# Four paddings between matmul operands in SBUF, in a fused retention, maxout and bilinear kernel

## The chip, the cores and the metric

The kernel runs on one core of one Trainium2 chip. The metric is device time in microseconds (us) for one launch, the median of several runs. An effect of under 0.5%, about 6.35 us here, can't be told from no change by such runs.

## The reference, cut to what matters

```
scores = (q @ k^T) / sqrt(64), decayed by gamma_h ** (i - j) for j <= i     # 8 batches, 8 heads, 576 positions, width 64
x = scores @ v                          -> [4608, 512]
h = max(x @ w1, x @ w2, x @ w3)         -> [4608, 768]     (first products)
z = h @ w_out                           -> [4608, 512]
g = (z @ u1) * (z @ u2)                 -> [4608, 1024]
out = g @ (u3 @ u_out)                  -> [4608, 512]     (the kernel folds u3 and u_out into one matrix, w4)
```

The inputs are float32, the weights come as 64-bit words. Each float32 operand is split into a high and a low part in the matmul type float32r, and a product is three matmuls: high by high, low by high, high by low.

## The kernel before

The work runs in stages, and TensorE (PE) has matmuls in nearly all of it:

- 0 to 569 us: attention by chunks of 64 or 128 positions, mixed with the **first products** (line 486). A first product is 12 matmuls of 128x128 weights (the stationary operand, `w1h` and `w1l`, pool `w1`) against 512 columns of `xh` and `xl` (the moving operand, pools `x0` to `x2`). 166 products make 1992 matmuls, 1896 of them 512 columns wide and 96 (the halved ones at the start) 256 wide. `ORDER` and the due times of `when` set the sequence.
- 569 to 698 us: **z** in seven products per group of tokens (a Strassen-like scheme, `Z_ORDER`), stationary `zp["w"]` (`za11h` and so on), moving `hh`, `hl` from a ring of three (line 772, `product` at line 709). Four groups are 512 wide (504 matmuls), the last is 256 wide (126 matmuls) and reads columns 48 to 304 of its tiles (`columns`, line 116).
- 698 to 896 us: **the fold of the last two weights into w4** (192 matmuls of 512 columns into `ps_w`, stationary `th`, `tl`, moving `oh`, `ol`, pool `t34`), then the products for g (`ps_x`, `ps_v`, `ps_y`, stationary the sums in `wsum`, moving `ops`): 1344 matmuls of 512 columns and, from 897 to 936 us, 336 of 256 columns.
- 1089 to 1264 us: **the output products**, 1512 matmuls of 256 columns, stationary the pieces of g, moving the pieces of w4.

Tiles lie in SBUF where their pools put them: a pool's tiles follow each other in the order in which they are first asked for, pools on the left side grow upward and on the right side downward. Nearly all tiles of operands are a whole number of 256 bytes per partition, so all stationary operands of a stage share one remainder of the address modulo 256, and all moving ones another. Below, the **offset** of a matmul is the start of the weights loaded for the next matmul less the start of its own moving operand, modulo 256. In the program as built before the change it is 0 for all first products, for z and for the fold into w4 at 512 columns and for the products for g at 512 columns; it is 64 for the last group of z, the last group of the products for g and all output products. Three places of the code set it already: `skew(o_p, 352)` at line 801, `columns`, and the `skew` of 32 or 64 bytes at line 1034.

Of the kernel before, what the change touches and what calls it, by code (L numbers as in the profile page):

```python
# [9 lines left out]
F32 = mybir.dt.float32  # L10
# [12 lines left out]
P = 128  # L23
# [64 lines left out]
def tile_retention_maxout_bilinear(ctx: ExitStack, tc, a, out):  # L88
# [3 lines left out]
    def copy_r(dst, src):  # L92
        nc.scalar.activation(dst, src, AF.Copy)  # L93

    def low(eng, dst, full, hi):
        eng.tensor_tensor(dst, full, hi.bitcast(F32), ALU.subtract)  # L96
# [13 lines left out]
    g_d = [dram.tile([P, KF2, N1], F32, name=f"g_d{t}") for t in range(NT // N1)]  # L110
    w4_d = dram.tile([P, KF2, DM], F32, name="w4_d")

    def skew(pool, size):
        pool.tile([P, size // 4], F32, name="skew")

    def columns(size):
        at = 0 if size == N1 else 48
        return slice(at, at + size)
# [2 lines left out]
        return ps_mm.tile([P, 512], F32, tag="mm", name=name)  # L121

    left = ctx.enter_context(ExitStack())
    hb_p = left.enter_context(tc.tile_pool(name="hb", bufs=4, side="left"))
    w1_p = left.enter_context(tc.tile_pool(name="w1", bufs=1, side="left"))
    x_p = {2: left.enter_context(tc.tile_pool(name="x2", bufs=1, side="left"))}
    cv_x = ctx.enter_context(ExitStack())
    x_p.update({t: cv_x.enter_context(tc.tile_pool(name=f"x{t}", bufs=1, side="left")) for t in range(2)})
    cv = cv_x.enter_context(tc.tile_pool(name="cv", bufs=2, side="left"))
# [372 lines left out]
    for t in range(n_blk):  # L502
        for f in range(KF1):
            for i in range(3):
                k = T_BLK * t + 3 * f + i
                if t < EARLY:
                    split = t == 0 and 3 * f + i < HALVED
                    for e, cols in enumerate(halves if split else (whole,)):
                        name = f"{t}.{3 * f + i}" + "ab"[e] * split
# [12 lines left out]
    zp = {}  # L522
# [7 lines left out]
    def splitter(pool, src, hi, lo, eng, tag, bufs):  # L530
        raw = pool.tile([P, hi.shape[-1]], F32, tag=tag, name=tag, bufs=bufs)
        load(raw, src)

        def split():
            copy_r(hi, raw)
            low(eng, lo, raw, hi)

        return split

    def open_z():  # L540
        right.close()
        cv_x.close()
        zp["ps"] = ctx.enter_context(tc.tile_pool(name="ps_2", bufs=2, space=PSUM, side="right"))
        p = zp["p"] = bx.enter_context(tc.tile_pool(name="zp", bufs=1, side="right"))
        zp["w"] = {x: [p.tile([P, KH, half], F32R, name=f"z{x}{v}") for v in "hl"] for x in AN}

    def raw_h(tag, bufs=1):
        return zp["p"].tile([P, KH, N1], F32, tag=tag, name=tag, bufs=bufs)
# [56 lines left out]
    def split_h(n):  # L605
        j, n = divmod(n, len(Z_ORDER))
        if j < len(z_groups):
            x = Z_ORDER[n][1]
            raw, size = hr[j, x], z_groups[j][3]
            hh, hl = hq[j, n] = [zp["p"].tile([P, KH, N1], F32R, tag=f"h{v}", name=f"h{v}", bufs=Z_RING)[:, :, columns(size)] for v in "hl"]  # L610
            copy_r(hh, raw)
            low(nc.vector, hl, raw, hh)

    t_last = T_BLK * (n_blk - 1)
    when(t_last, open_z)
    for c, tag in enumerate(("T3", "T2", "b21")):
        for n, step in enumerate(z_weights(c, tag)):
# [7 lines left out]
    for n in range(Z_RING):  # L625
        when(t_last + 13.6 + n, split_h, n)
    when(t_last + 15.2, load_h, 1, "b11")

    with tc.manual_schedule():
# [88 lines left out]
        t34, w3t, wo2 = {}, {}, {}  # L718
# [4 lines left out]
            return splitter(t34["p"], flat(w3t_d[:, k, 4 * e:4 * e + 4]), *map(flat, w3t[n]), nc.vector, "raw34", 3)  # L723

        def get_wo2(k):
            wo2[k] = [t34["p"].tile([P, DM], F32R, tag=x, name=x) for x in ("oh", "ol")]
            return splitter(t34["p"], wo2_d[:, k], *wo2[k], nc.gpsimd if k % 2 else nc.vector, "raw34", 3)

# [2 lines left out]
        def prepare_34(*gets):  # L731
            for split in pending:
                split()
            pending[:] = [get(n) for get, n in gets]

        first_34 = [((get_w3t, 0), (get_wo2, 0)), ((get_w3t, 1),), ((get_w3t, 2), (get_wo2, 1)), ()]

        def open_34():
            t34["p"] = t34x.enter_context(tc.tile_pool(name="t34", bufs=2, side="left"))

        zo_p = bx.enter_context(tc.tile_pool(name="zo", bufs=1, side="right"))

# [16 lines left out]
        for j, (_, _, _, size) in enumerate(z_groups):  # L759
            Z = {}  # L760
            saved = {}
            for n, (x, y) in enumerate(Z_ORDER):
                bank_of = "XVXYXYX"[n]
                fresh = bank_of not in Z
                if fresh:
                    Z[bank_of] = [bank8(f"ps_{bank_of}{i}") for i in range(2)]
                ps = Z[bank_of]
                ah, al = zp["w"][x]
                bh, bl = hq.pop((j, n))
                for i in range(2):  # L770
                    ms = slice(i * P, i * P + P)
                    product(ps[i][:, :size], [(ah[:, c, ms], al[:, c, ms], bh[:, c], bl[:, c]) for c in range(KH)], fresh, True, not fresh)
                for i in range(2):
                    if n in (0, 2, 3):
                        saved[n, i] = snap_z(ps[i], size)
                    elif n == 6:
                        keep_z(j, 2 + i, 0, ps[i])
                    else:
                        keep_z(j, *{1: (i, 0), 4: (2 + i, 1), 5: (i, 1)}[n], ps[i], saved.pop(({1: 0, 4: 3, 5: 2}[n], i)))
                split_h(j * len(Z_ORDER) + n + Z_RING)  # L780
                for fn, dj, *args in behind_z[n]:
                    fn(j + dj, *args)
                if steps and n in (2, 3, 5, 6):
                    steps.pop(0)()
            if j == 3:
                for step in steps:
                    step()
                sx.close()
                open_34()
                steps = [lambda gets=gets: prepare_34(*gets) for gets in first_34]  # L790
# [8 lines left out]

        ops = [operand_set(o_p, 0)]  # L800
        skew(o_p, 352)
        behind = []

# [79 lines left out]
        for n in range(2 * KF2):  # L883
            k, e = divmod(n, 2)
            th, tl = w3t.pop(n)
            for m in range(4 * e, 4 * e + 4):
                if k == 0:
                    ps_w.append(bank8(f"ps_w{m}"))
                product(ps_w[m], [(th[:, m % 4], tl[:, m % 4], *wo2[k])], k == 0, k == KF2 - 1)
                if k == KF2 - 1:  # L890
                    t = w4_p.tile([P, DM], F32, tag="w4", name="w4")
                    copy_r(t, ps_w[m])
                    load(w4_d[:, m], t)
            prepare_34(*[(get_w3t, n + 3)] * (n + 3 < 2 * KF2), *[(get_wo2, k + 2)] * (e == 1 and k + 2 < KF2))
            lows()
            if steps:
                steps.pop(0)()
# [120 lines left out]
        def g_steps(s):  # L1018
# [13 lines left out]
            def split(x, eng):  # L1032
                if s in (0, 3) and not ops:
                    skew(gpool[s % 2], 32 if s else 64)
                h, l = ops[x] = [gpool[s % 2].tile([P, 4, P], F32R, tag=f"{x}{v}", name=f"{x}{v}") for v in "hl"]
                src = w[x]
                copy_r(h, src)
                if s:
                    low(eng, l, src, h)
                else:  # L1040
                    behind.append(lambda: low(eng, l, src, h))
# [58 lines left out]
        for n, (k, q) in enumerate(visits):  # L1100
            B, size = ops[k % 2], z_groups[k][3]
# [190 lines left out]
```

## Time and profile before

| | |
|---|---|
| median of 3 runs | 1270.91 us (1267.66 to 1272.45) |
| the profiled execution's own time | 1266.24 us |
| its span, first to last instruction | 1264.5 us |
| PE busy | 1256.5 us, 99% of the span |
| granted TensorE clock | 1.000 in the mean: 2.4 GHz throughout |
| DVE, ACT, POOL busy | 882.8, 487.2, 314.5 us |

How to read it: matmuls are pipelined, so a row's length ("mean ns of one") is longer than the distance from one matmul's start to the next. In an undisturbed stretch of matmuls of one shape the length less about 162 ns is that distance. A weight load (LDWEIGHTS, engine PEld) has rows of its own, and runs beside the matmul before the one it serves.

### The profile page before, as it was taken

What the parts mean: (1) busy time and instruction counts of PE and PEld (TensorE: products, weight loads), DVE (VectorE), ACT (ScalarE), POOL (GpSimd) and SP (SyncE); (2) the same over time, 40 slices, a digit from 0 to 9 for tenths busy, and PEclk for the clock granted to TensorE, in tenths of its full rate; (3) what the DMA queues carried; (4) which work ended last, traced back from release to release, by engine and by line L of the source; (5) the groups of instructions that cost most, each with busy time, mean ns of one, the idle gap of its engine ahead of it and who ended that gap; (6) DMA issues with size and microseconds to landing.
All of it is one profiled execution on the core that took longest, in us unless ns stands there. A gap on an engine that the chain in (4) does not pass through costs nothing.

```text
span 1264.5 us, 22993 instructions
## 1 busy us (share of the span) xinstructions
PE 1256.5 (99%) x8900; PEld 1078.9 (85%) x8900; DVE 882.8 (70%) x1256; ACT 487.2 (39%) x873; POOL 314.5 (25%) x262
## 2 busy tenths in 40 slices
PE   9999999999999999999999999999999999999999
PEld 6888888888888888888888788888998888999998
DVE  5985666666666766366898446776666766899896
ACT  4541122222222222234565354443344343455554
POOL 2201211211111110000000314544243542344443
PEclk9999999999999999999999999999999999999999
DMA  9945787787878895434743643333333315355553
GB/s 219 239 115 118 151 221 195 184 213 177 239 183 177 179 197 148 159 108 166 226 158 125 219 128 121 122 119 108 106 113 133 117 51 162 131 175 159 168 174 101
DMA packets 323793, 199.34 MB, mean 158 GB/s; under 512 B 241634, under 2 KB 279266, under 8 KB 323684
## 3 DMA queue, kind: packets, MB, share of 16 engines
q1 hardware_dynamic: 323684, 197.87, 56.7%
q8 instruction: 70, 1.15, 0.4%
q14 instruction: 39, 0.32, 0.1%
HBM read 131.76 MB, written 66.06 MB: 156 GB/s over the span
## 4 chain that ended last, share of the span: by engine, by line
PE 94%; DVE 3%; DMA 2%; ACT 1%; issue 1%; SPq 0%; POOL 0%; DVEq 0%; ACTq 0%; POOLq 0%
PE ps_h L486 35%; PE ps_x L715 23%; PE ps_y L715 11%; PE ps_v L715 6%; PE ps_X L715 5%; PE sc L369 3%; PE o L384 3%; PE ps_w L715 2%; PE ps_Y L715 2%; PE st L404 1%; PE ps_V L715 1%; PE o L391 1%; DMA raw<-w3t_d 1%; DMA a<-wp_d 1%; PE kp L345 0%
## 5 line engine op out<-in xcount | busy, mean ns | idle before, releaser
L486 PE MATMUL ps_h<-xh,w1h 128*128 128x512 f32 (+1 forms) x664 | 257.5, 389 | 0.0
L486 PE MATMUL ps_h<-xh,w1l 128*128 128x512 f32 (+1 forms) x664 | 254.4, 385 | 0.4 <-DVE w1l L96 0.4
L486 PE MATMUL ps_h<-xl,w1h 128*128 128x512 f32 (+1 forms) x664 | 174.2, 384 | 0.0
L486 PEld LDWEIGHTS ps_h<-xh,w1h 128*128 128x128 f32 x664 | 124.6, 188 | 27.6 <-issue 2.1
L486 PEld LDWEIGHTS ps_h<-xh,w1l 128*128 128x128 f32 x664 | 124.8, 188 | 24.7 <-DVE w1l L96 0.6
L486 PEld LDWEIGHTS ps_h<-xl,w1h 128*128 128x128 f32 x664 | 123.0, 188 | 24.8
L496 DVE TENSOR_TENSOR hb<-ps_h,hb 128x512 f32<-128x512 f32 (+1 forms) x110 | 74.4, 676 | 97.5 <-PE ps_h L486 92.6
L1146 POOL TENSOR_TENSOR c<-c 128x512 f32<-128x512 f32 (+1 forms) x60 | 83.4, 1391 | 176.7 <-DVE c L1138 123.3
L1133 ACT ACTIVATE snap<-ps_x 128x512 f32<-128x512 f32 (+1 forms) x100 | 55.5, 555 | 176.5 <-PE ps_x L715 175.7
L355 POOL TENSOR_TENSOR q<-q,tables 128x512 f32<-128x512 f32 (+1 forms) x31 | 31.4, 1012 | 276.4 <-DMA q<-in_q_dram 209.1
L93 ACT ACTIVATE hb<-ps_h 128x512 f32<-128x512 f32 (+1 forms) x56 | 32.5, 580 | 148.9 <-PE ps_h L486 139.1
L166 ACT ACTIVATE e<-raw 128x512 f32<-128x512 f32 x64 | 42.8, 669 | 105.8 <-DMA raw<-in_moe_w_dram 67.3
L93 ACT ACTIVATE xh<-o 128x512 fp32r<-128x512 f32 (+1 forms) x40 | 22.2, 554 | 118.8 <-PE o L391 76.9
L96 POOL TENSOR_TENSOR ol<-raw,oh 128x512 fp32r<-128x512 f32 x4 | 6.5, 1636 | 239.5 <-DVE tl L96 219.0
L358 POOL TENSOR_TENSOR v<-v,tables 128x512 f32<-128x512 f32 x40 | 44.6, 1117 | 59.9 <-DMA v<-in_v_dram 55.3
L376 DVE TENSOR_TENSOR p<-sc,mask 128x512 f32<-128x512 f32 (+1 forms) x80 | 48.0, 627 | 11.8 <-PE sc L369 11.7
L1138 DVE TENSOR_TENSOR c<-ps_x,snap 128x512 f32<-128x512 f32 (+1 forms) x40 | 25.2, 637 | 38.8 <-PE ps_x L715 15.9
L172 DVE CUSTOM_DVE_ANT_0 m<-m,r 128x1024 uint16<-128x1024 uint16 x64 | 47.0, 735 | 6.9
L1138 DVE TENSOR_TENSOR c<-ps_v,snap 128x512 f32<-128x512 f32 (+1 forms) x40 | 25.0, 635 | 35.2 <-PE ps_v L715 19.7
L715 PE MATMUL ps_x<-t4h,a 128*128 128x512 f32 (+1 forms) x160 | 45.5, 368 | 0.3 <-DVE a L96 0.3
L715 PE MATMUL ps_x<-b11h,a 128*128 128x512 f32 (+1 forms) x160 | 45.2, 367 | 0.0
L715 PE MATMUL ps_y<-b22h,s 128*128 128x512 f32 (+1 forms) x160 | 45.2, 367 | 0.0
(299 smaller groups left out, 3262.5 us busy)
## 6 DMA issues: line engine op xcount, KB each, us to landing
zr<-g_d SPq DMA_DIRECT2D x18, 1024.0 KB, 6.1
raw<-in_moe_w_dram SPq DMA_DIRECT2D x34, 512.0 KB, 5.7
g_d<-c SPq DMA_DIRECT2D x64, 256.0 KB, 2.1
zr<-z_d SPq DMA_DIRECT2D x28, 512.0 KB, 6.2
h_d<-hb SPq DMA_DIRECT2D x54, 256.0 KB, 3.4
b<-h_d SPq DMA_DIRECT2D x16, 768.0 KB, 6.6
out_dram<-ob SPq DMA_DIRECT2D x35, 256.0 KB, 2.0
v<-in_v_dram SPq DMA_DIRECT2D x32, 256.0 KB, 4.2
```

Of the source, the lines that this page charges most:

```text
L93: nc.scalar.activation(dst, src, AF.Copy)
L166: nc.scalar.activation(z["e"], raw[:, :, 1].bitcast(F32), AF.Copy, scale=2.0 ** -112)
L172: nc.vector.tensor_tensor(z["m"], z["m"], z["r"], ALU.add)
L358: nc.gpsimd.tensor_tensor(z["v"], z["v"], vd.unsqueeze(2).to_broadcast([P, H, D]), ALU.mult)
L369: nc.tensor.matmul(z["sc"][g][keys, h, :c], z["kt"][rows, h, keys], z["qt"][rows, h, :c], start=True, stop=True)
L376: nc.vector.tensor_tensor(z[g][:c, :, :c], z["sc"][g][:c, :, :c], mask[:c, :c].unsqueeze(1).to_broadcast([c, G, c]), ALU.mult)
L486: nc.tensor.matmul(ps[:, cols], l, r, start=n == 0, stop=n == len(mms) - 1)
L496: nc.vector.tensor_tensor(hb, ps[:, cols], hb, ALU.max)
L715: nc.tensor.matmul(ps, l, r, start=start and j == 0, stop=stop and j == len(mms) - 1, skip_group_check=again)
L1133: nc.scalar.activation(t, ps[:, :size], AF.Copy)
L1138: nc.vector.tensor_tensor(r, ps[:, :size], t, ALU.add)
L1146: nc.gpsimd.tensor_tensor(x, x, y, ALU.mult)
```

## The change

`skew` makes a dummy tile that moves the tiles behind it. It gets a numbered name and one buffer (`bufs=1`), and is called in six new places, in the pools `w1`, `x2`, `zp` (twice) and `t34` (twice):

```
--- before.py
+++ after.py
-    def skew(pool, size):
-        pool.tile([P, size // 4], F32, name="skew")
...
     left = ctx.enter_context(ExitStack())
+    skews = []
+
+    def skew(pool, size):
+        skews.append(pool.tile([P, size // 4], F32, name=f"skew{len(skews)}", bufs=1))
+
     hb_p = left.enter_context(tc.tile_pool(name="hb", bufs=4, side="left"))
     w1_p = left.enter_context(tc.tile_pool(name="w1", bufs=1, side="left"))
+    skew(w1_p, 192)
     x_p = {2: left.enter_context(tc.tile_pool(name="x2", bufs=1, side="left"))}
+    skew(x_p[2], 64)
...
         zp["w"] = {x: [p.tile([P, KH, half], F32R, name=f"z{x}{v}") for v in "hl"] for x in AN}
+        skew(p, 192)
...
             hh, hl = hq[j, n] = [zp["p"].tile([P, KH, N1], F32R, tag=f"h{v}", name=f"h{v}", bufs=Z_RING)[:, :, columns(size)] for v in "hl"]
+            if j == 0 and n == 0:
+                skew(zp["p"], 96)
...
         def get_wo2(k):
+            if k == 0:
+                skew(t34["p"], 192)
             wo2[k] = [t34["p"].tile([P, DM], F32R, tag=x, name=x) for x in ("oh", "ol")]
...
         def open_34():
             t34["p"] = t34x.enter_context(tc.tile_pool(name="t34", bufs=2, side="left"))
+            skew(t34["p"], 64)
```

In the program as built, the offsets become:

| matmuls | count | offset before | after |
|---|---|---|---|
| first products, 512 and 256 columns | 1896 and 96 | 0 | 192 (64 below) |
| z, 512 columns | 504 | 0 | 64 |
| z, last group, 256 columns | 126 | 64 | 128 |
| fold into w4, 512 columns | 192 | 0 | 64 |
| products for g, 512 and 256 columns | 1344 and 336 | 0 and 64 | the same |
| output products, 256 columns | 1512 | 64 | the same |

No instruction is added, removed or moved: on every engine and on SP's queue the built programs hold the same operations in the same order with the same waits. Only addresses in SBUF differ.

## Rows read from the trace of the kernel before

**Rows 1.** The page: busy time by engine, granted clock, chain that ended last.
```profile
PE 1256.5 (99%) x8900; PEld 1078.9 (85%) x8900; DVE 882.8 (70%) x1256; ACT 487.2 (39%) x873; POOL 314.5 (25%) x262
...
PEclk9999999999999999999999999999999999999999
...
PE 94%; DVE 3%; DMA 2%; ACT 1%; issue 1%; SPq 0%; POOL 0%; DVEq 0%; ACTq 0%; POOLq 0%
PE ps_h L486 35%; PE ps_x L715 23%; PE ps_y L715 11%; PE ps_v L715 6%; PE ps_X L715 5%; PE sc L369 3%; PE o L384 3%; PE ps_w L715 2%; PE ps_Y L715 2%; PE st L404 1%; PE ps_V L715 1%; PE o L391 1%; DMA raw<-w3t_d 1%; DMA a<-wp_d 1%; PE kp L345 0%
```

**Rows 2.** Groups by line and shape, whole span: 512 columns.
```profile
line engine op names shapes xcount | busy us, mean ns | idle before us <-releasers
L486 PE MATMUL ps_h<-xh,w1h 128*128 128x512 f32 x632 | 248.8, 394 | 0.0
L486 PE MATMUL ps_h<-xh,w1l 128*128 128x512 f32 x632 | 246.2, 390 | 0.0
L486 PE MATMUL ps_h<-xl,w1h 128*128 128x512 f32 x632 | 169.0, 389 | 0.0
...
L715 PE MATMUL ps_w<-oh,th 128*128 128x512 f32 x64 | 25.2, 394 | 0.3 <-ACT oh L93 0.3
```

**Rows 3.** Groups by line and shape, 509 to 568 us: first products.
```profile
L486 PE MATMUL ps_h<-xh,w1h 128*128 128x512 f32 x88 | 34.3, 389 | 0.0
```

**Rows 4.** Groups by line and shape, 571 to 683 us: z.
```profile
L715 PE MATMUL ps_V<-hh,za12h 128*128 128x512 f32 x24 | 9.3, 389 | 0.0
```

**Rows 5.** Groups by line and shape, 42.2 to 44 us: halved first products.
```profile
L486 PE MATMUL ps_h<-xh,w1l 128*128 128x256 f32 x6 | 1.5, 283 | 0.0
L486 PE MATMUL ps_h<-xl,w1h 128*128 128x256 f32 x7 | 1.2, 283 | 0.0
```

**Rows 6.** Groups by line and shape, 684 to 697 us: z's last group.
```profile
L715 PE MATMUL ps_X<-hh,zs3l 128*128 128x256 f32 x6 | 1.7, 281 | 0.0
```

**Rows 7.** Groups by line and shape, 897 to 925 us: last group for g.
```profile
L715 PE MATMUL ps_x<-t2h,s 128*128 128x256 f32 x24 | 4.4, 281 | 0.0
```

**Rows 8.** Groups by line and shape, 927 to 936 us: the same matmuls, later.
```profile
L715 PE MATMUL ps_v<-b21h,a 128*128 128x256 f32 x8 | 1.4, 276 | 0.0
```

**Rows 9.** Groups by line and shape, 1112 to 1260 us: output products.
```profile
L715 PE MATMUL ps_x<-wt,s3h 128*128 128x256 f32 x64 | 13.5, 276 | 0.0
```

**Rows 10.** Busy time by stretch: us, each engine's busy us (instructions), clock, DMA share, GB/s.
```profile
897.00:925.00 28.00, 28.00 (x241) 28.00 (x240) 20.73 (x38) 13.58 (x32) 7.46 (x9) 1.00 0.18 62
...
940.00:1088.00 148.00, 148.00 (x654) 122.57 (x653) 102.54 (x129) 63.09 (x115) 62.53 (x42) 1.00 0.33 110
1089.00:1100.00 11.00, 11.00 (x95) 11.00 (x94) 8.71 (x15) 4.88 (x10) 2.33 (x2) 1.00 0.43 144
1112.00:1260.00 148.00, 148.00 (x1308) 148.00 (x1307) 128.05 (x166) 78.89 (x168) 65.42 (x46) 1.00 0.49 156
```

**Rows 11.** Timeline, 247.3 to 248 us: start, duration, engine; a first product before attention.
```profile
247.13 0.61 PE L486 MATMUL ps_h<-xl,w1h 128*128 128x512 f32 x2
247.13 0.19 PEld L486 LDWEIGHTS ps_h<-xl,w1h 128*128 128x128 f32 x1
...
247.67 0.43 PEld L404 LDWEIGHTS st<-v,kn 128*64 128x64 f32 x12 [0.35 <-issue]
```

**Rows 12.** Groups by line and shape, 247.55 to 247.65 us: the last of those alone.
```profile
L486 PE MATMUL ps_h<-xl,w1h 128*128 128x512 f32 x1 | 0.4, 388 | 0.0
```

**Rows 13.** Timeline of PE, 124 to 128.5 us: first products after attention.
```profile
126.25 0.50 PE L486 MATMUL ps_h<-xh,w1h 128*128 128x512 f32 x1
126.58 0.39 PE L486 MATMUL ps_h<-xh,w1l 128*128 128x512 f32 x1
126.81 0.40 PE L486 MATMUL ps_h<-xh,w1h 128*128 128x512 f32 x1
```

## Prediction

> **What bounds the kernel now.** I read the page first, then the groups by line and shape, then stretches of time. PE is busy for 99% of the span at the full clock, 2.4 GHz in every slice, and the chain that ended last is PE for 94%, the first products alone for 35% [rows 1]. So time comes or goes only with the distance from one matmul to the next, and the reader is to look at lengths of matmuls. At 512 columns they are 389 ns in the first products and in z [rows 3, 4]. At 256 columns there are three lengths: 283 ns in the halved first products (offset 0), 281 ns in z's last group and at first in g's last group (offset 64), and 276 ns later in that group and in the output products (offset 64 too) [rows 5 to 9]. How a length stands to a distance: from 940 to 1088 us there are 654 matmuls in 148.00 us, about 227 ns apart, and from 1112 to 1260 us 1308, about 113 ns apart [rows 10]; the lengths there are 389 and 276, both 162 to 163 more. So 281 and 283 mean 5 and 7 ns more per matmul than 276.
>
> **What the offset did so far.** Rows 5 to 9 are what speaks for such paddings: with offset 0 a 256-column matmul took 7 ns over the shortest, with offset 64 either 5 ns over or nothing. Which of the two it is does not follow from the offset alone, since g's last group has both with the same offsets [rows 7, 8]. A weight load is 0.19 us long [rows 11]: at 256 columns, 113 ns apart, there is always one under way, at 512 columns, 227 ns apart, there is time without one.
>
> **The change part by part.** The change moves no instruction and no wait, so it has one term only: a price per matmul times the matmuls whose offset changes. These are 1896 first products, 504 of z and 192 of the fold into w4 at 512 columns, 2592 together, and at 256 columns 96 first products and 126 of z.
>
> *512 columns, what can be gained.* If a clash between the weight load and the moving operand were in the 389 ns, a matmul without a weight load beside it would be shorter. The trace has such matmuls: where attention takes over, the last first product has nothing beside it. In rows 11 a pair of them begins at 247.13, so the second begins 0.23 us later at 247.36, and the next weight load comes only at 247.67, 0.31 us behind that start [rows 11]. It is 388 ns long [rows 12], against 389 with a load [rows 3]. So at offset 0 the load costs 1 ns, and the most that a better offset can give is 2592 x 1 ns = 2.6 us. The columns themselves are the rest: 388 less 276 is 112 ns for 256 more columns, so 512 columns take about 224 ns with no load near.
>
> A rule of the Trainium skill bears on this (TensorE: Matmul & The Clock Gate, section "Step-by-step: what each phase is for"): loading the next weights takes no SBUF read bandwidth from the running matmul, since PE reads the two through separate ports. By that rule every offset is as good as another and the sum is 0. The 1 ns at 512 columns agrees with it; the 5 and 7 ns at 256 columns don't, so it isn't taken for granted for new offsets.
>
> *512 columns, what can be lost.* No row shows 512 columns at an offset of 64 or 192. The nearest rows are the 256-column ones, with 5 and 7 ns. For the 696 of z and of the fold (offset 64) the rows at that offset give 0 or 5 ns: 0 to 3.5 us. For the 1896 first products (offset 192) there is no row at all: 0 to 7 ns, or 0 to 13.3 us. I take 0 for both: at 512 columns the load ends long before the matmul, so what it loses in a clash can be made up within the same matmul, and the long stretches at 512 columns show that PE falls into the undisturbed distance of 227 ns by itself after a few matmuls. That can be seen behind each pause: the first is 0.50 us long, the next ones 0.39 to 0.40 [rows 13], and in the quiet stretch at the end it is 389 for all [rows 3].
>
> *After a pause.* The first products' groups have 394, 390 and 389 ns in the mean over the span [rows 2], 632 x (5 + 1) ns = 3.8 us over 389. There are 22 returns from attention, and the first matmul of each is 0.11 us longer, 2.4 us, because its follower's weights are loaded late; padding doesn't touch this. What is left, 1.4 us, is the few matmuls that settle. Another offset may shorten or lengthen this: -1.4 to +1.4 us, taken as 0.
>
> *256 columns.* The 96 halved first products go from 283 to an unknown length, at best 276: -0.7 us at most, and much of that is hidden since PE waits for weights there. z's last group goes from 281 to 276 at best, 126 x 5 = -0.6 us, or to 283, +0.3 us. Taken as 0.
>
> *What isn't padded but may follow.* g's last group begins at 281 and the output products too: 241 and 95 matmuls [rows 7, 10]. If they inherit another rhythm from the stage ahead and begin at 276, that is -1.2 and -0.5 us. Taken as 0.
>
> Sum: 0. Against the profiled execution that is 1266.2 us again (span 1264.5 and 1.7 us around it). That execution lies 4.7 us below the median of the runs, so as a time to be measured I take the median, **1270.9 us**. All gains together are 2.6 + 1.4 + 0.7 + 0.6 + 1.2 + 0.5 = 7.0 us, to 1263.9; the losses that still belong to this case are 3.5 us (z and the fold at 5 ns), 1.4 and 0.3: 5.2 us, to 1276.1.
>
> **The rivals.**
>
> *The first products clash at 192 (slower).* The mechanism: at 64 below, the weight load of the next matmul and the moving operand meet in a way that repeats in each matmul, as at 256 columns with offset 0, where it doesn't go away, and PE never reaches the distance of 227 ns. For it: at 256 columns the offset does matter, and 64 below is a place that no row covers. Against it: the slack at 512 columns, and the 1 ns. Its price is 1896 x 5 to 7 ns = 9.5 to 13.3 us, 1280.4 to 1284.2; with z and the fold in the same state 2592 x 5 to 7 = 13.0 to 18.1 us, 1283.9 to 1289.0. It decides from 6.35 us / 1896 = 3.4 ns per first product.
>
> *What lies over 2.4 GHz is clash after all (faster).* 512 columns at 2.4 GHz are 213 ns, the rows show 227, and if all of the 14 ns over that came from operands that meet and the new offsets ended it, 2592 x 14 = 36 us would go: 1235 us. Against it stands the 388 ns of the matmul without a load, and that 256 columns more take 112 ns where 2.4 GHz would make 107. It would need the lone matmul to be slowed by something else. [...]
>
> *The change doesn't do what it says.* The built program has the offsets of the text, so this is left as: the relation modulo 256 between these two starts is not what made 283, 281 and 276. Then nothing moves, which is the forecast's time.
>
> **How the numbers follow.** Forecast (no offset matters at 512 columns by more than 1 to 2 ns): 0.58, 1270.9 us, its own range 1263.9 to 1276.1. Slower by the first products' clash, with or without the others: 0.36, 1280 to 1289. Faster by over 0.5%: 0.06, nearly all of it the second rival or several small gains at once. What a measurement can tell from no change is about 0.5%, 6.35 us. The range runs from 1264, all small gains, to 1284, the upper price of the clash in the first products alone; outside it are the cases of all three stages at 7 ns and of the large gain.
>
> **What would show it.** Right: the first products' groups stay at 388 to 390 ns in a quiet stretch, z's and the fold's at 389, PE's lone matmul before attention at 388, DVE, ACT and POOL as before, the clock 2.4 GHz throughout. The clash: the first products' three groups at 394 to 396 in the stretch that now has 389, with PE's idle time unchanged and the whole difference between 0 and 569 us. The gain: 375 to 378 there. A different length in z than in the first products would show that the sign of the offset counts. The forecast is wrong if any 512-column group moves by over 3 ns; it is right for a wrong reason if two groups move against each other.

## The result: 0.6% slower, and the profile after

| | before | after |
|---|---|---|
| median of the runs taken side by side | 1268.12 us (11 runs, 1264.33 to 1272.45) | 1273.9 us (11 runs) |
| ratio after to before, 95% interval | | 1.0056 (1.0034 to 1.0078) |
| profiled execution, and its span | 1266.24, 1264.5 us | 1278.55, 1276.8 us |

One execution of after, at 1791.95 us, and one of before, at 5968.75 us beside the last two whole kernels below, were disturbed and are left out of the ratios and spreads. The other ten of after lie between 1271.79 and 1280.1 us. The kernel became slower, by little more than a measurement can tell; the forecast was no change.

The page of after: busy time by engine, granted clock in 40 slices, chain that ended last by engine.

```profile
PE 1268.9 (99%) x8900; PEld 1084.6 (85%) x8900; DVE 885.8 (69%) x1256; ACT 489.1 (38%) x873; POOL 312.3 (24%) x262
...
PEclk9999999999999999999999999999999999999999
...
PE 97%; DVE 2%; DMA 1%; ACT 1%; issue 0%; POOL 0%; ACTq 0%; DVEq 0%; POOLq 0%
```

Against [rows 1] PE is busy 12.4 us longer with the same 8900 instructions, and the span is 12.3 us longer; DVE, ACT and POOL are within 3 us of what they were, and the clock is 2.4 GHz throughout. So the time lies in PE's own distances. The groups by line and shape tell where, here in quiet stretches (515 to 565 us, 600 to 680, 684 to 697, 725 to 750, 800 to 890, 1120 to 1268); the matmuls of L486 and L715 stand at L491 and L723 in after.

```profile
L491 PE MATMUL ps_h<-xh,w1h 128*128 128x512 f32 x74 | 29.0, 392 | 0.0
L491 PE MATMUL ps_h<-xh,w1l 128*128 128x512 f32 x74 | 28.9, 391 | 0.0
...
L723 PE MATMUL ps_V<-hh,za12h 128*128 128x512 f32 x18 | 7.1, 396 | 0.0
...
L723 PE MATMUL ps_X<-hl,zs2h 128*128 128x256 f32 x6 | 1.7, 282 | 0.0
...
L723 PE MATMUL ps_w<-ol,th 128*128 128x512 f32 x37 | 14.6, 396 | 0.0
...
L723 PE MATMUL ps_y<-b22h,s 128*128 128x512 f32 x40 | 12.3, 389 | 0.0
...
L723 PE MATMUL ps_x<-wt,s2h 128*128 128x256 f32 x64 | 13.9, 281 | 0.0
```

The first products went from 389 to 391 and 392 [rows 3], z from 389 to 396 [rows 4], z's last group from 281 to 282 [rows 6], the fold into w4 reads 396 too. The products for g, whose offset did not change, still read 389. The last row is the surprise: the output products, not touched by the change, read 281 where they read 276 [rows 9]. The counts in equal stretches say the same. Here are the stretches of 50, 80, 25 and 148 us by busy time, first of after, then of before (first bracket: PE's matmuls).

```profile
515.00:565.00 50.00, 50.00 (x220) 41.03 (x219) 26.75 (x51) 13.89 (x29) 0.00 (x0) 1.00 0.43 143
600.00:680.00 80.00, 80.00 (x344) 64.51 (x343) 70.94 (x64) 45.61 (x53) 0.00 (x0) 1.00 0.53 175
725.00:750.00 25.00, 25.00 (x109) 20.13 (x108) 15.24 (x18) 12.58 (x23) 6.98 (x5) 1.00 0.47 141
...
1112.00:1260.00 148.00, 147.78 (x1256) 147.58 (x1255) 128.66 (x167) 78.18 (x165) 65.39 (x45) 1.00 0.50 160
```

```profile
515.00:565.00 50.00, 50.00 (x222) 41.39 (x222) 27.86 (x50) 14.91 (x31) 0.00 (x0) 1.00 0.46 154
600.00:680.00 80.00, 80.00 (x355) 66.26 (x354) 72.97 (x67) 45.53 (x53) 0.00 (x0) 1.00 0.55 178
725.00:750.00 25.00, 25.00 (x112) 20.68 (x111) 12.03 (x18) 13.95 (x25) 3.48 (x2) 1.00 0.48 154
```

80 us hold 344 matmuls of z where they held 355, and 148 us hold 1256 output products where they held 1308 [rows 10]. From here on I give the **distance** from one matmul's start to the next, taken from the records in stretches without a pause. The stages, by the start of each stage's first matmul in the two profiled executions:

| stage | us before | us after | difference | distances before and after, ns |
|---|---|---|---|---|
| until the first full product | 49.24 | 47.63 | -1.6 | |
| first products, mixed with attention | 519.98 | 524.49 | +4.5 | 227.1, 229.0 |
| z, 512 columns | 114.74 | 117.71 | +3.0 | 226.7, 233.3 |
| z, last group | 14.84 | 14.96 | +0.1 | 117.8, 118.7 |
| fold into w4 | 45.73 | 46.13 | +0.4 | 227.5, 233.3 |
| products for g | 344.41 | 344.42 | 0.0 | 226.7, 226.7 (512 columns) |
| output products to the end | 175.59 | 181.50 | +5.9 | 113.3, 117.8 |

The table adds up to the 12.3 us. Stages that are the same also differ between profiled executions: with the first products at offset 0 that stage took 520.0, 520.4, 520.6 and 522.1 us in four kernels, and z at offset 0 114.5 to 115.9. So single differences of the table carry 1 to 2 us, and the distances are the steadier measure. By distances times matmuls the changed offsets are worth 1873 x 1.93 = 3.6 us in the first products (those that another follows at once), 504 x 6.67 = 3.4 in z, 192 x 5.8 = 1.1 in the fold, 0.1 in z's last group: **8.2 us**. The stages of the table give 4.5 + 3.0 + 0.1 + 0.4 = 8.0. The -1.6 at the start and the +5.9 at the end remain. The start took 47.5 to 49.2 us in the eight profiled executions of whole kernels here, before and after lie near its two ends, and no run tells whether the padding has a part in that. The experiments had to tell whether the +5.9 belongs to the change.

### The profile page after: what moved, and what is told of

Same layout as the page of the kernel before. It is cut to its first block, busy times and chain, and to the rows that moved or that the text cites. A ratio compares the mean times of both kernels' runs of the same rounds, so it can differ in the third digit from the quotient of the medians.

```text
span 1276.8 us, 22993 instructions
## 1 busy us (share of the span) xinstructions
PE 1268.9 (99%) x8900; PEld 1084.6 (85%) x8900; DVE 885.8 (69%) x1256; ACT 489.1 (38%) x873; POOL 312.3 (24%) x262
## 4 chain that ended last, share of the span: by engine, by line
PE 97%; DVE 2%; DMA 1%; ACT 1%; issue 0%; POOL 0%; ACTq 0%; DVEq 0%; POOLq 0%
PE ps_h L491 35%; PE ps_x L723 23%; PE ps_y L723 11%; PE ps_X L723 6%; PE ps_v L723 6%; PE ps_Y L723 3%; PE ps_w L723 3%; PE sc L374 3%; PE o L389 3%; PE ps_V L723 1%; PE st L409 1%; PE o L396 1%; DMA raw<-w3t_d 1%; PE kp L350 0%; DVE zr L1055 0%; PE qp L350 0%
## 5 line engine op out<-in xcount | busy, mean ns | idle before, releaser
L491 PE MATMUL ps_h<-xh,w1h 128*128 128x512 f32 (+1 forms) x664 | 258.5, 391 | 0.0
L491 PE MATMUL ps_h<-xh,w1l 128*128 128x512 f32 (+1 forms) x664 | 255.4, 386 | 0.0
L491 PE MATMUL ps_h<-xl,w1h 128*128 128x512 f32 (+1 forms) x664 | 175.7, 386 | 0.0
L491 PEld LDWEIGHTS ps_h<-xh,w1h 128*128 128x128 f32 x664 | 124.7, 188 | 28.6 <-issue 2.1
L491 PEld LDWEIGHTS ps_h<-xh,w1l 128*128 128x128 f32 x664 | 124.8, 188 | 25.3
L491 PEld LDWEIGHTS ps_h<-xl,w1h 128*128 128x128 f32 x664 | 123.0, 188 | 25.9
L180 DVE SCALAR_TENSOR_TENSOR m<-raw,m 128x512 int32<-128x512 int32 x64 | 45.8, 720 | 0.2
L723 PE MATMUL ps_x<-t4h,a 128*128 128x512 f32 (+1 forms) x160 | 45.5, 368 | 0.3 <-DVE a L96 0.3
L723 PE MATMUL ps_x<-b11h,a 128*128 128x512 f32 (+1 forms) x160 | 45.2, 367 | 0.0
```

The lines of the kernel that those rows point to most:

```text
L180: nc.vector.scalar_tensor_tensor(z["m"], z["hi"], -0x80000000, z["m"], ALU.bitwise_and, ALU.bitwise_or)
L491: nc.tensor.matmul(ps[:, cols], l, r, start=n == 0, stop=n == len(mms) - 1)
L723: nc.tensor.matmul(ps, l, r, start=start and j == 0, stop=stop and j == len(mms) - 1, skip_group_check=again)
```

## The experiments

**Matmuls alone, one offset after another.** This kernel has nothing of the reference's work, only blocks of 60 (512 columns) or 90 (256) matmuls.

```
for cols, offs, shift, count, blocks in PLAN:      # offs: 0, 16, ... 240
    ...
    for i in range(count):
        w = offs[i % len(offs)] // 4 + N1 * (i % 3)
        x = shift // 4 + N1 * (i // 3 % 3)
        nc.tensor.matmul(ps[:, :cols], sta[:, w:w + P], mov[:, x:x + cols], ...)
```

> Only matmuls, none of the reference's work: blocks of 60 matmuls of 512 columns or 90 of 256 columns, float32r, each with its own 128x128 weights, a pause between blocks, and the offset (start of the weights less start of the moving operand, modulo 256 bytes) stepped by 16 from 0 to 240. Also 512 columns at offsets 0 and 64 with both operands moved by 64 bytes, and weights that alternate between offset 0 and 64 or 0 and 192. Theory A (the offset alone sets the settled distance from matmul to matmul): 512 columns give 227 ns at 0, 233 at 64, 229 at 192 in every block, the same with both operands moved, and other values at the other offsets; 256 columns give 120 at 0, 113 or 118 at 64, 119 at 128, 118 at 192. Theory B (the distance is a rhythm that one stage hands to the next or that a pause sets by chance): blocks of one offset differ among themselves as much as blocks of different offsets, and 512 columns at 64 come back to 227 ns in some blocks.

Groups of the second half of a block each (28.36 to 36.07 us, 192.88 to 200.81, 567.46 to 575.24, 745.51 to 753.22, 917.75 to 925.42, 1147.45 to 1154.71); in a name, n is the columns, s the bytes by which both operands are shifted, o where the weights start.

```profile
L44 PE MATMUL n512s0o0b<-mov,sta 128*128 128x512 f32 x36 | 8.3, 389 | 0.0
...
L44 PE MATMUL n512s0o64b<-mov,sta 128*128 128x512 f32 x36 | 8.6, 395 | 0.0
...
L44 PE MATMUL n512s0o192b<-mov,sta 128*128 128x512 f32 x35 | 8.2, 391 | 0.0
...
L44 PE MATMUL n512s64o64b<-mov,sta 128*128 128x512 f32 x36 | 8.3, 389 | 0.0
...
L44 PE MATMUL n256s0o0b<-mov,sta 128*128 128x256 f32 x66 | 8.1, 283 | 0.0
...
L44 PE MATMUL n256s0o64b<-mov,sta 128*128 128x256 f32 x67 | 7.8, 276 | 0.0
```

389, 395 and 391 are, to 1 ns, the lengths that before and after have in their stages, with no other engine at work beside PE: the offset alone makes them. Both operands moved by 64 bytes (fourth row, offset 0) read 389 again, and at offset 64 moved so 233.3 ns apart again, so it is the relation of the two starts and not the place of either. The distances in ns:

| offset | 0 | 16 to 64 | 80 | 96 | 112 to 160 | 176 | 192 | 208 | 224 | 240 |
|---|---|---|---|---|---|---|---|---|---|---|
| 512 columns | 226.7 | 233.3 | 232.0 | 234.3 | 233.3 or 233.4 | 230.1 | 228.9 | 231.7 to 233.3 | 233.3 | 226.7 or 228.3 |

| offset | 0 | 16, 32 | 48 | 64 | 80 to 96 | 112, 144, 160 | 128 | 176, 192 | 208, 224 | 240 |
|---|---|---|---|---|---|---|---|---|---|---|
| 256 columns | 120.0 | 118.3 | 117.8 to 123.3 | 113.3 | 117.3 to 118.8 | 120.0 | 118.7 | 117.8 to 118.1 | 116.7, one block 117.8 | 117.3, one block 120.0 |

At the offsets that the kernels use at 512 columns (0, 64 and 192) all blocks of an offset agree: there theory A (the offset sets the distance, and the distance stays) holds and B falls. It isn't so at every offset: at 512 columns the blocks at 208 and at 240 differ among themselves, and 128 gave 233.3 here and 232.4 in the last sweep below; at 256 columns those at 48, 96, 224 and 240 differ. No offset is better than 0 at 512 columns, and 64 is the best at 256: what before already had. At 64 and 192 the distance doesn't fall back to 227 by itself within 60 matmuls. Weights that alternate between offsets 0 and 64 gave 232.5, 230.0 and 230.0 ns in three blocks, and between 0 and 192 230.0 in all three, more than the mean of 226.7 and 228.9: the price is not simply a sum over single matmuls.

**The first products' paddings alone.**

```
+    skew(w1_p, 192)
...
+    skew(x_p[2], 64)
```

> Only the first products' padding (offset 192), z and the fold into w4 back at 0. Theory A: first products at about 229 ns in quiet stretches (length 391 to 392), z and the fold back at 227 (389); 1873 x 2.2 ns less what the shorter settling gives back, about +3.6 us over the kernel before, ratio 1.003. Theory B: z and the fold stay at 233 ns since they follow slower first products, +8 us, ratio 1.006.

Measured: 1272.31 us against 1270.59 for before, ratio 1.0025 (1.0000 to 1.0050), the profiled execution 3.3 us over that of before. First products in 515 to 565 us, z in 600 to 680, the fold in 725 to 750:

```profile
L491 PE MATMUL ps_h<-xh,w1h 128*128 128x512 f32 x73 | 28.6, 392 | 0.0
...
L720 PE MATMUL ps_V<-hh,za12h 128*128 128x512 f32 x18 | 7.0, 389 | 0.0
...
L720 PE MATMUL ps_w<-oh,th 128*128 128x512 f32 x34 | 13.2, 389 | 0.0
```

The first products keep their 229.0 ns, z and the fold are back at 389. The twelve executions fall into two halves, 1267.64 to 1269.92 and 1274.70 to 1277.04, some 6 us apart: as much as the output products' 5.9, though only one of the twelve has a profile to show which it had.

**z's and the fold's paddings alone**, that is, the other four `skew` calls of the change.

> Only the paddings of z and of the fold into w4 (offset 64, z's last group at 128), first products back at 0. Theory A: z and the fold at 233 ns (length 395 to 396), 504 x 6.7 + 192 x 5.8 ns = 4.5 us over the kernel before, ratio 1.0035; first products at 227. Theory B: z and the fold back at 227 ns and the time that of before, ratio 1.000.

Measured: 1274.96 us, ratio 1.0028 (1.0004 to 1.0052). The same stretches:

```profile
L489 PE MATMUL ps_h<-xh,w1h 128*128 128x512 f32 x75 | 29.2, 389 | 0.0
...
L721 PE MATMUL ps_V<-hh,za12h 128*128 128x512 f32 x18 | 7.1, 396 | 0.0
...
L721 PE MATMUL ps_w<-oh,tl 128*128 128x512 f32 x33 | 13.1, 396 | 0.0
```

The other half of the change, with z and the fold at 233.3 and 233.4 ns. This profiled execution had its output products at 117.8; less 5.9 us it is 3.7 over before. So the parts, 3.3 and 3.7 us in single executions, make up most of the 8, and 1.0025 and 1.0028 add up to 1.0053, near the 1.0056 of the whole.

**The signs changed over**: first products at 64, z and the fold at 192, z's last group at 0.

```
-    skew(w1_p, 192)
+    skew(w1_p, 64)
...
-    skew(x_p[2], 64)
+    skew(x_p[2], 192)
...
-        skew(p, 192)
+        skew(p, 64)
...
-                skew(t34["p"], 192)
+                skew(t34["p"], 64)
...
-            skew(t34["p"], 64)
+            skew(t34["p"], 192)
```

> The change with the signs exchanged: first products at offset 64, z and the fold at 192, z's last group at 0. Theory A: first products at 233 ns, 1896 x 6.6 = 12.5 us, z and the fold at 229 ns, 696 x 2.2 = 1.5 us, z's last group at 120 ns, 126 x 2.2 = 0.3 us: +14 us over the kernel before, ratio 1.011. If 64 bytes apart costs the same whichever operand is above, or the stage and not the offset sets the price: first products +3.6, z and fold +4.5 as in the change, ratio 1.006.

Measured: 1281.5 us, ratio 1.0093 (1.0061 to 1.0125), nearer to the 1.011 of theory A than to 1.006. The first products, 515 to 565 us:

```profile
L491 PE MATMUL ps_h<-xh,w1h 128*128 128x512 f32 x71 | 28.4, 399 | 0.0
L491 PE MATMUL ps_h<-xh,w1l 128*128 128x512 f32 x70 | 27.5, 393 | 0.0
L491 PE MATMUL ps_h<-xl,w1h 128*128 128x512 f32 x68 | 18.6, 396 | 0.0
```

That is 396 in the mean. Distances: first products 233.3, z 228.9, the fold 230.2, z's last group 120.0. Each stage took the distance that its offset has in the sweep (the fold 1 ns more), not one of its own. The signs of the change were the cheaper choice of the two, since the offset of 192 fell to the stage with the most matmuls.

**What sets the output products' two rhythms** (a rhythm is a distance that lasts). Again only matmuls: 30 of 512 columns, then 24 of 256 at an offset that varies, then 60 of 256 at 64, without a pause; and twice without the part in the middle.

```
PLAN = [((512, 0, 30), (256, off, 24), (256, 64, 60)) for off in range(0, 256, 16)]
PLAN += [((512, 0, 30), (256, 64, 60)), ((512, 64, 30), (256, 64, 60))]
```

> Only matmuls, none of the reference's work: 30 of 512 columns at offset 0, then without a pause 24 of 256 columns at an offset from 0 to 240 in steps of 16, then 60 of 256 columns at offset 64; three blocks of each. Last, 512 columns at offset 0 or 64 straight into 256 columns at 64. Theory C (at 256 columns and offset 64 there are two lasting rhythms, 113.3 and 117.8 ns, and the one that is met depends on what ran just before, not on chance): every block straight from 512 columns at offset 0 settles at 117.8, and each offset in between leads to the same one of the two in its three blocks, some to 113.3. Rival D (chance): the three blocks of one offset differ.

The last 40 matmuls of three blocks, all at 64: behind 24 at offset 0 (19.91 to 24.39 us), behind 24 at 32 (126.38 to 130.69), straight behind 512 columns (861.67 to 866.15).

```profile
L45 PE MATMUL n512o0an256o0an256o64b<-mov,sta 128*128 128x256 f32 x41 | 5.0, 281 | 0.0
...
L45 PE MATMUL n512o0an256o32an256o64b<-mov,sta 128*128 128x256 f32 x40 | 4.7, 276 | 0.0
...
L45 PE MATMUL n512o0an256o64b<-mov,sta 128*128 128x256 f32 x41 | 5.0, 281 | 0.0
```

117.8, 113.3 and 117.8 ns, with the same matmuls at the same addresses in all three. Straight behind 512 columns it was 117.8 in all six blocks; behind 24 matmuls at 32, 80, 96, 128, 144, 160 or 192 to 240 it was 113.3 in all blocks, behind 0, 16, 48, 64, 112 or 176 it was 117.8 in all. So at 256 columns and offset 64 there are two lasting distances, and what runs ahead picks one (theory C): the difference that rows 7 and 8 showed.

In the kernel PE stops once about 21 us into the output products. The timelines of PE there (start, duration, line; idle time in brackets), of before and of after:

```profile
1109.68 0.28 PE L715 MATMUL ps_v<-wb,a12h 128*128 128x256 f32 x1
1110.19 0.39 PE L715 MATMUL ps_x<-kt,a22h 128*128 128x256 f32 x1 [0.23 <-DVE ob L1214]
```

```profile
1116.09 0.28 PE L723 MATMUL ps_v<-wb,a12h 128*128 128x256 f32 x1
1116.59 0.38 PE L723 MATMUL ps_x<-kt,a22h 128*128 128x256 f32 x1 [0.22 <-DVE ob L1225]
```

In both, the distance is 113.3 ns ahead of the stop. Behind it, before goes on at 113.3 and after at 117.8, to the end; the restart came 511 ns behind the last start in the one and 500 ns in the other. Of the three runs above, the one with z's and the fold's paddings restarted after 500 ns too and went on at 117.8; the other two had 117.8 ahead of it, restarted after 159 and 162 ns and went on at 113.3. These five would fit a rhythm picked by the moment of the restart. But the changed kernel with a shift (below) had 113.3 ahead, restarted after 501 ns and went on at 113.3, with no shifted product near: the moment, as far as the records resolve it, does not decide alone. What picks the rhythm at this stop stays open.

**Before without that stop**: one of VectorE's preparing steps moved behind two sums.

```
-                prepare(2 if s else 3)
+                prepare({0: 3, 1: 1}.get(s, 2))
...
-                prepare(2 if s else 3)
+                prepare(2 if s > 1 else 3)
```

> The kernel before with one VectorE operation of the output products moved behind two others (the fourth difference of the second piece of g goes behind the sums that free a PSUM bank), so that PE doesn't stop for 0.4 to 0.5 us some 21 us into the output products. Theory C: without that stop the rhythm in which PE enters its last 1330 matmuls is the one it had by the 100th, so runs lie nearer to each other; where it is 113.3 ns the time is 1265 to 1267 us, where it is 117.8 it is 5.9 us more. If the stop makes the choice by chance and the wait before it does so too, the spread of 12 us stays, and the median moves by 0.4 us only.

Measured: 1271.76 us (1264.95 to 1275.22) against 1266.81, ratio 1.0017 (0.9992 to 1.0042). The stop went, the spread of the runs didn't. 1114 to 1254 us by busy time:

```profile
1114.00:1254.00 140.00, 140.00 (x1191) 140.00 (x1190) 120.86 (x156) 74.25 (x157) 60.83 (x43) 1.00 0.50 159
```

1191 matmuls in 140 us are 117.6 ns: the slow rhythm, entered without any stop there. Theory C had expected the runs to lie nearer to each other, and that missed. The rhythm can change at the stop, but it is also set ahead of it.

**Before, with the rhythm set by a shift.** The sweep of entries says what picks 113.3 ns: some matmuls at 224 ahead of those at 64. The first product of z's last group, of each quarter of g's last group, and at three places of the output products (from their first, 73rd and 241st matmul on) has an offset of 224 instead; no instruction is added or moved.

```
...
-    def columns(size):
-        at = 0 if size == N1 else 48
+    def columns(size, first=False):
+        at = 0 if size == N1 else 8 if first else 48
...
-                h, l = ops[x] = [gpool[s % 2].tile([P, 4, P], F32R, tag=f"{x}{v}", name=f"{x}{v}") for v in "hl"]
+                room, at = (64, 40 * (s in (0, 1, 3))) if x == "a11" else (0, 0)
+                h, l = ops[x] = [gpool[s % 2].tile([P, 4 * P + room], F32R, tag=f"{x}{v}", name=f"{x}{v}")[:, at:at + 4 * P].rearrange(
+                    "p (k t) -> p k t", k=4) for v in "hl"]
...
```

> The kernel before with the first product of some 256-column stages put at offset 224 instead of 64: z's last group (18 matmuls), g's last group (4 times 12) and the first, second and fourth piece of the output products (12 each); the same instructions in the same order. Theory C: at 224 about 116.7 ns, and from there PE enters offset 64 in the rhythm of 113.3 ns, so z's last group and g's last group stay at 113.3 ns behind it (length 276 instead of 281) and the output products from the fourth piece on in every run. Against a run of the kernel before that has 113.3 ns there: about -0.4, -1.0 and -0.3 us; against one that has 117.8 ns: 5.9 us more. Median 4 to 5 us below that of before, ratio 0.9965, and runs within 3 us of each other instead of 12. Rival D: by chance as before, ratio 1.000, same spread.

Measured: 1265.47 us (1264.29 to 1269.53) against 1267.42, ratio 0.9982 (0.9966 to 0.9998): below before, if only just, by 2 us where 4 to 5 were expected. 1150 to 1250 us of its output products, and the same stretch of after, by busy time:

```profile
1150.00:1250.00 100.00, 100.00 (x885) 100.00 (x884) 89.44 (x118) 55.37 (x118) 45.64 (x32) 1.00 0.51 163
```

```profile
1150.00:1250.00 100.00, 100.00 (x851) 100.00 (x850) 86.41 (x112) 52.62 (x111) 43.63 (x31) 1.00 0.51 160
```

885 against 851 in 100 us; the profiled execution of before had 885 as well. Nine of its twelve executions lie within 1264.3 to 1266.6 us, where before's, taken side by side, spread from 1263.98 to 1274.43. Two parts missed: z's last group and the first quarter of g's last group stayed at 117.8 in spite of their first product at 224. The shift of the sweep does not carry over everywhere.

**The change, with the rhythm set in the same way** (not in z's last group, which is at 128 there).

> The changed kernel with the same shift at g's last group and the output products (not in z's last group, whose offset the change moves to 128). Theories A and C: with the output products' rhythm fixed, what is left between this and the kernel with the shift alone is the change's own price: first products 1873 x 1.9 = 3.6 us, z and the fold 504 x 6.7 + 192 x 5.8 = 4.5 us, z's last group 126 x 118.7 against 18 x 116.7 + 108 x 113.3 = 0.6 us: 8.7 us, ratio to the kernel before about 1.003 to 1.004. If the change's price came from the output products' rhythm, the two would be alike.

Measured: 1272.82 us (1271.45 to 1275.66), ratio to before 1.0038 (1.0023 to 1.0054). Its output products from 1150 to 1250 us, by busy time:

```profile
1150.00:1250.00 100.00, 100.00 (x885) 100.00 (x884) 89.77 (x117) 54.78 (x116) 44.53 (x31) 1.00 0.53 168
```

885 again, 113.3 ns. With the rhythm the same in both profiled executions, and no execution of the one within the range of the other, the change costs 1272.82 - 1265.47 = 7.35 us: that is its own price, next to 8.2 by distances (8.7 expected). The 5.9 us of the profiled execution are not the change's.

**Is it the load, column by column?** Only matmuls: at 512 moving columns weights of 128, 96, 64 and 32 columns, then 448, 384 and 320 moving columns with weights of 128.

```
nc.tensor.matmul(ps[:m, :cols], sta[:, w:w + m], mov[:, x:x + cols], ...)
```

> Only matmuls, none of the reference's work: 512 moving columns with weights of 128, 96, 64 or 32 columns at offsets 0, 64, 128 and 192, then 448, 384 and 320 moving columns with weights of 128. Theory E (the price of an offset comes from the weight load that runs beside the matmul, column against column): at 64 the 6.7 ns over offset 0 fall with the width of the weights, to about 3.3 ns at 64 columns and 1.7 at 32, and at 448 to 320 moving columns they stay near 6.7. Theory F (it comes from how the start of one matmul stands to the end of the one before, whatever runs beside): 6.7 ns or another amount that does not fall in step with the width of the weights, and it changes irregularly with the number of moving columns.

| | offset 0 | 64 | 128 | 192 |
|---|---|---|---|---|
| 512 columns, weights of 128 | 226.7 | 233.3 | 232.4 | 228.9 |
| weights of 96 | 230.0 | 228.3 to 233.4 | 231.7 | 233.4 |
| weights of 64 | 230.0 | 231.1 to 232.6 | 229.2 to 231.1 | 228.4 |
| weights of 32 | 231.7 | 231.7 | 230.3 to 230.9 | 231.1 to 231.7 |
| 448 columns, weights of 128 | 202.7 | 202.2 | 203.9 | 200.0 |
| 384 columns | 173.3 | 176.7 | 176.1 | 173.3 |
| 320 columns | 146.7 | 146.7 | 146.7 | 146.7 |

Groups of half a block, weights of 32 at offset 0 (547.5 to 555.15 us) and 384 columns at 0 and at 64 (880.95 to 886.67, 914.97 to 920.8):

```profile
L42 PE MATMUL n512m32o0b<-mov,sta 128*32 128x512 f32 x35 | 8.3, 394 | 0.0
...
L42 PE MATMUL n384m128o0b<-mov,sta 128*128 128x384 f32 x34 | 6.1, 334 | 0.0
L42 PE MATMUL n384m128o64b<-mov,sta 128*128 128x384 f32 x35 | 6.3, 338 | 0.0
```

A quarter of the weights reads 394 where all of them read 389. What 64 costs over 0 does shrink with the width of the weights, 6.7 ns at 128 columns and none at 32, but because offset 0 gets dearer, and at 448, 384 and 320 moving columns it is -0.5, 3.3 and 0 ns where theory E wanted about 6.7. If each loaded column that meets the moving operand cost something, fewer columns would cost less; that (theory E) falls. That the distance hangs on how a matmul's start falls against the end of the one before (theory F) agrees with the irregular table, but F forecast no amounts that could have failed, and no run shows what meets there: why an offset costs what it does stays open.

## Why the prediction was wrong

**What bounds the kernel, and the one term** were right: PE alone, at 2.4 GHz, other engines of no account; the term is a price per matmul times a count. The forecast fell on the price.

**What can be gained** was bounded at 1 ns per matmul, 2.6 us, and nothing did gain: no offset of the sweep goes below 226.7 ns at 512 columns, so the rival of 36 us falls as well. But the bound was reached by an inference that doesn't hold: that the lone matmul's 388 ns [rows 12] is what a matmul takes with no load beside it. In after, one of these lone matmuls (around 187.5 us) reads

```profile
L491 PE MATMUL ps_h<-xl,w1h 128*128 128x512 f32 x1 | 0.4, 397 | 0.0
```

and of the 22 lone ones ahead of attention 17 read 397 and 5 read 388, with nothing loaded beside them in either kernel. All 22 read 388 in before. It is not a matter of the recorded end alone: where a lone matmul reads 397 the next weight load begins some 325 ns behind its start, where it reads 388 some 317 ns. So the length follows from more than a load beside it, and 389 against 388 says nothing on what another offset costs.

**What can be lost** is the step that failed: "0 to 3.5 us" for z and the fold, "0 to 13.3" for the first products, "I take 0 for both", since "what it loses in a clash can be made up within the same matmul" and PE "falls into the undisturbed distance of 227 ns by itself". PE does settle behind a pause, but at the distance of the offset: 233.3 ns at 64, 228.9 at 192, for as long as the block lasts. A return to 227 at offset 0 [rows 13] could show only the level of offset 0. By distances the terms were 4.5 us for z and the fold, over the upper end of 3.5, since 6.7 ns are more than the 5 that the 256-column row lent; and 3.6 us for the first products, at the lower part of 0 to 13.3. That the measured 1273.9 us lies within the forecast's own range, 1263.9 to 1276.1, is luck: the price, 7 to 8 us, is over the 5.2 us of losses that the range allows for, and the base of 1270.9 was 2.8 too high.

By the rule of the Trainium skill that the prediction weighed (TensorE: Matmul & The Clock Gate, "Step-by-step: what each phase is for": the load of the next weights takes no read bandwidth from the running matmul) offsets would have cost nothing. The sweep's 226.7 against 233.3 decides against reading it so, though it doesn't show that reads are what is lost.

**The rival of a clash in the first products** had the mechanism, a pattern that repeats in each matmul and doesn't go away, but the wrong size and place: 5 to 7 ns were taken from 256 columns, the rows gave 2 at 192, under its own threshold of 3.4; z and the fold had the 7. 1280 to 1284 us was not reached, since the dear offset fell to 696 matmuls and the cheap one to 1896. "The forecast is wrong if any 512-column group moves by over 3 ns" was met by z and the fold, which moved by 7; the sign of the offset counts, as a different length in z was to show.

**Small terms.** z's last group was taken at 0 between -0.6 and +0.3 us and cost 0.1. The inherited rhythm was counted as a possible gain alone, 1.2 and 0.5 us. That the 276 of the output products [rows 9] was itself one of two rhythms, and could be lost for 5.9 us, was missed, although rows 7 and 8 showed both at the same offsets. It accounts for nearly half of the 12.3 us between the two profiled executions, and is not the change's. The median of more runs of before, 1268.12 us, lies 2.8 below the base that was taken.

## What to carry to other kernels

Where PE's distance from matmul to matmul is the bound, lay out nothing by reasoning on addresses: run the stage's own shape alone at every offset, several blocks each, since at some offsets blocks differ, and read the settled distance. An offset that is best for one width (64 at 256 columns) can be among the worst for another (512). And when a stage that a change doesn't touch differs between two profiles, look for a lasting state that each execution enters on its own, set it in both kernels, and compare again.

## What the runs showed of the chip beyond that

- The settled distance in these matmuls depends on the start of the weights against the start of the moving operand modulo 256: at 512 columns 226.7 to 234.3 ns, at 256 columns 113.3 to 120.0 with two blocks at 123.3, at 320 columns 146.7 at all four offsets tried. At a few offsets, 208 and 240 at 512 columns among them, blocks of the same offset settle differently.
- At 256 columns and offset 64 two distances last, 113.3 and 117.8 ns, for over 1300 matmuls in a row; in the sweep the matmuls run ahead decide between them, in the kernel what decides is shown only in part.
- The plain distances are whole multiples of 6.67 ns (113.3, 120.0, 146.7, 173.3, 226.7, 233.3), and others repeat over a few matmuls, whose sum is again such a multiple (117.8 x 3 = 353.3 and 228.9 x 3 = 686.7). What that step is, no run shows.
